# Carried-state exponents from DRAM as repeated rows, and a new order of round 2, in a fused scan and feed-forward kernel

## The chip, the cores and the metric

The kernel runs on one core of one Trainium2 chip. The metric is the device time of one execution in microseconds, as the median of several runs. TensorE does the matrix products, VectorE, ScalarE and GpSimd the element-wise work, SyncE issues DMAs. Products land in PSUM, which has eight banks of 128 x 512 floats here.

## The reference

First a gated linear recurrence in chunks over 4 batches, 8 heads, 768 steps, with head dimension 32 and state dimension 16; then a feed-forward layer with a leaky ReLU over the 3072 tokens of width 256 and inner width 2048.

```python
la = log(clip(a, 1e-6, 1));  cum = cumsum(la)            # per chunk
M = (C @ B.T) * exp(cum_i - cum_j) * causal
y = M @ x  +  (C @ state) * exp(cum_i)                   # exp(cum_i): exponents of the carried state
state = exp(sum(la)) * state + sum_j (B_j x_j) * exp(cum_last - cum_j)
h = y_as_tokens @ w_in;  out = maximum(0.01 * h, h) @ w_out
```

The kernel may choose its own chunk length; it takes 64 steps, so 12 chunks.

## The kernel before, in words

`scan_ffn` sets down every instruction in the order in which its engine runs it (`tc.manual_schedule()`): each engine goes through its own list in program order, and waits between engines follow from the tiles. Its first part is the scan, with the feed-forward work woven in; its second part is feed-forward alone.

The scan has a prologue, which makes the row sums of the decays and does chunks 0 and 1, and then rounds c = 2 to 12 (the loop `for c in range(2, NC + 1)`). Round c prepares chunk c + 1, computes the scores of chunk c and the output of chunk c - 1:

- `decays(c + 1, h)`, a product for each half h of the decay matrix, into the bank `dspace(c + 1, h)`; `decay_exp` takes its exponent on ScalarE. Up to chunk 3 the halves go to the banks `pd` and `HB[0]`, later both go to `pd`.
- `scores(c)` into the banks `pa` and `pb`; `weigh(c, half)` multiplies them on VectorE with the decays (first `pb`, then `pa`).
- `passed(c + 1)`, two products that repeat the chunk's row sums (`er`, three bf16 parts of each, through the 0/1 matrix `esel`) over the 16 state rows of each head; `passed_exp` takes their exponent on ScalarE into `es`, 128 x 256.
- `weigh_c(c + 1)` on GpSimd: `es` times C. `end_decay(c)` on GpSimd: the old state times the last exponent of the chunk. `weigh_b(c)` on GpSimd: B times its decays.
- `states(c - 1)`: the state update of a chunk; up to round 3 into `o01`, columns 128 to 191 of each of its quarters of 256, later into `pb`. `keep_state(c - 1)` copies it on VectorE in two instructions, added to `end_decay`'s product.
- `outputs(c - 1)`: y into the last 64 columns of the quarters of `pa` and `pb`. `keep_out` copies it on ScalarE (high part, two instructions), `low_out` takes the rest on VectorE (up to round 4).
- In rounds 2 and 3 there is no feed-forward product yet; `keep_warm(10, o01[:, 1, :2 * Q])` and `keep_warm(4, o01[:, 1])` put ten and four filler products without use there. From round 4 on `ffn_in(f, 0, HB[0])` and `ffn_out` stand there.
- `decode(c, part)`: the steps that turn 64-bit weights into pairs of floats: magnitude on ScalarE (L107), clamp, shift, sign and low bits on VectorE (L110, L115, L121, L127), high part on ScalarE (L133), rest on GpSimd (L136).

In round 2 VectorE moreover makes the second third of the row sums' parts (`split(1, sum1)`, four instructions), fills a slot of `dr` (`fill_slots`, L272) and copies mask rows (`mask_rows(5, NC)`, L417); ScalarE copies sign rows (`sign_rows(5, NC)`, L411). The parts are saved to DRAM (`save_sums`) and come back as rows of `dr`, `dl` and `er` (`send_rows`, `send_cols`, `send_er`).

Loads stand on SyncE's queue in program order, each as soon as its buffer is free: in every round `bs`, half of a weight (`raw`), `cs`, the other half, `ts` and `xs`.

Of the kernel before, what the change touches and what calls it, by code (L numbers as in the profile page):

```python
# [10 lines left out]
F32 = mybir.dt.float32  # L11
F32R = mybir.dt.float32r
BF16 = mybir.dt.bfloat16
U32 = mybir.dt.uint32
AF = mybir.ActivationFunctionType
# [19 lines left out]
KD = PR + 3 * GB  # L35
NE = 3 * NH
DIRECT = 2
SLOTS = 5
WARM = 6
FIRST = 4  # L40
# [9 lines left out]
def scan_ffn(ctx: ExitStack, tc: tile.TileContext, a_l, bcn_l, x_l, w_l, out_l):  # L50
# [145 lines left out]
    espace, zlate = (v[:, :, 2 * Q:2 * Q + 2 * D] for v in quarters)  # L196

    def dspace(c, h):
        return (pd, HB[0] if c < FIRST else pd)[h]

    early_q = o01.rearrange("p s (a x) -> p (s a) x", a=NH2)

    def exspace(c):
        return espace if c > 2 else early_q[:, :, (c + 1) * Q:(c + 2) * Q]
# [23 lines left out]
    dr = cst.tile([128, SLOTS, GB, Q], BF16, name="dr")  # L228
    erev = cst.tile([128, NC * GB], F32, name="erev")
    esel = cst.tile([NE, 128], BF16, name="esel")  # L230
    er = cst.tile([NE, NC * 2, CT // 2], BF16, name="er")
    parts = [cst.tile([128, 3, 2 * Q], BF16, name=f"parts{i}") for i in range(2)]
    lax = cst.tile([128, GB, N], F32, name="lax")
    reach = [p3.tile([128, GB, Q], F32, name="lt") for _ in range(DIRECT)]
# [3 lines left out]
    sel = cst.tile([128, NG, 2], F32, name="sel")  # L238
    dram = open_pool(scan, "dram", space=bass.MemoryType.DRAM)
    sums = dram.tile([NC * GB, 3, 2 * Q], BF16, name="sums")  # L240

    bs, cs, ts, xs, cms, bnd, lts, es, cds, ss, tmps = ({} for _ in range(11))

    def fetch_bc(c, which):
        if c >= NC:
            return
        for i, (d, n) in enumerate(((bs, "bs"), (cs, "cs"), (ts, "ts"))):
            if n[0] in which:
                d[c] = pin.tile([128, CT], F32, name=n)
                sp.dma_start(d[c], bcn_l[c, :, i * CT:(i + 1) * CT])  # L250

    def fetch_x(c):
        if c < NC:
            xs[c] = pin.tile([128, GB, D], F32, name="xs")
            sp.dma_start(xs[c].rearrange("p g d -> p (g d)"), x_l[c])
# [15 lines left out]
    def fill_slots(lo, hi, copy):  # L271
        copy(dr[:KD, lo:hi], dr[:KD, SLOTS - 1:].to_broadcast([KD, hi - lo, GB, Q]))  # L272

# [76 lines left out]
    def fill_reach(c, h, eng):  # L350
        lo = c * GB + h * GB // 2
        eng.tensor_tensor(
            out=reach[c][:, halves[h]],
            in0=la[:, lo:lo + GB // 2].unsqueeze(2).to_broadcast([128, GB // 2, Q]),
            in1=seen.unsqueeze(1).to_broadcast([128, GB // 2, Q]), op=ALU.mult,
        )
# [21 lines left out]
    def split(i, space):  # L378
        n = (128, 64)[i]
        p, space = parts[i][:n], space[:n]  # L380
        dve.tensor_copy(p[:, 0], space)
        dve.tensor_tensor(out=rest[:n], in0=space, in1=p[:, 0], op=ALU.subtract)
        dve.tensor_copy(p[:, 1], rest[:n])
        dve.tensor_tensor(out=p[:, 2], in0=rest[:n], in1=p[:, 1], op=ALU.subtract)
# [19 lines left out]
    def send_er(lo, hi):  # L404
# [2 lines left out]
            sums[lo * GB:hi * GB].rearrange("(c k) p i -> (k p) c i", k=NH),  # L407
        )

    def sign_rows(lo, hi):  # L410
        act.copy(  # L411
            dl[ROW:PR, lo:hi],
            sign[ROW:PR, :2].unsqueeze(1).unsqueeze(3).to_broadcast([PR - ROW, hi - lo, 2, Q]),
        )

    def mask_rows(lo, hi):
        dve.tensor_copy(  # L417
            dl[:64, lo:hi].rearrange("p c h i -> p c (h i)"),
            upto_b.rearrange("p h i -> p (h i)").unsqueeze(1).to_broadcast([64, hi - lo, 2 * Q]),
        )  # L420
# [27 lines left out]
    def weigh(c, half):  # L448
        m = lts[c].rearrange("p (a g h) i -> p a g (h i)", a=NH2, g=NG)[:, :, 2 * half:2 * half + 2]
        dve.tensor_tensor(  # L450
            out=m, in0=sspace[half].rearrange("p g a x -> p a g x"), in1=m, op=ALU.mult,
        )
# [28 lines left out]

    def end_decay(c):
        tmps[c] = pw.tile([128, NB, 2, D], F32, name="tmp")
        e = es[c].rearrange("p (q i) -> p q i", q=NB)[:, :, Q - 1:]
        pool.tensor_tensor(
            out=tmps[c].rearrange("p q h d -> p q (h d)"),
            in0=ss[c - 1].rearrange("p q h d -> p q (h d)"),
            in1=e.to_broadcast([128, NB, 2 * D]), op=ALU.mult,
        )

    def weigh_b(c):
        bnd[c] = pw.tile([128, GB, N], F32, name="bnd")
# [6 lines left out]
    def decays(c, h):  # L499
        pe.matmul(  # L500
            dspace(c, h), lhsT=dl[:KD, c].rearrange("p h i -> p (h i)"),
            rhs=dr[:KD, slot(c), halves[h]].rearrange("p g i -> p (g i)"), start=True, stop=True,
        )
# [8 lines left out]

    def passed_exp(c):
        es[c] = p3.tile([128, CT], F32, name="es")
        act.activation(es[c].rearrange("p (q i) -> p q i", q=NB), exspace(c), AF.Exp)

    def weigh_c(c):
        cds[c] = p3.tile([128, CT], F32, name="cd")
        pool.tensor_tensor(out=cds[c], in0=es[c], in1=cs[c], op=ALU.mult)

    def outputs(c):
        mt, y = lts[c], [yspace(c, m) for m in range(2)]
# [49 lines left out]
    def decode(c, part):  # L572
        for g, f in duty[c, part]:
            g(f)
# [12 lines left out]
    sign_rows(2, 5)  # L587
    spread_c(0)
    fill_slots(0, 1, act.copy)
    fill_reach(1, 0, dve)  # L590
    fill_reach(1, 1, pool)
    pool.tensor_copy(
# [44 lines left out]
    passed_exp(2)  # L637
    fetch_bc(2, "t")
    fetch_x(2)
    fetch_bc(3, "bc")  # L640
    fetch_w(0)
    fetch_bc(3, "t")
# [3 lines left out]
    for c in range(2, NC + 1):  # L646
        f = c - FIRST
        if c + 1 < NC:
            alloc_lt(c + 1)
            decays(c + 1, 0)  # L650
            decay_exp(c + 1, 0)
        if c < NC:
            scores(c)
        if c < FIRST:
            states(c - 1)
        if c + 1 < NC:
            passed(c + 1)
            passed_exp(c + 1)
            decays(c + 1, 1)
        if c < NC:  # L660
            weigh(c, 1)
            weigh(c, 0)
        if c < NC - 1:
            weigh_b(c)
        if c + 1 < NC:
            spread_c(c + 1)
            decay_exp(c + 1, 1)
            weigh_c(c + 1)
        if c == 2:
            split(1, sum1)  # L670
            fill_slots(3, 4, dve.tensor_copy)
            mask_rows(5, NC)
            decode(1, 1)
            sign_rows(5, NC)
        if f >= 0:
            low = ffn_in(f, 0, HB[0])
        else:
            keep_warm(10, o01[:, 1, :2 * Q])
        decode(c, 0)
        if c == 3:  # L680
            send_rows(5, 7)
            send_er(5, NC)
            send_cols(5, NC, sp)
        fetch_bc(c + 2, "b")
        fetch_w(c + 3 - FIRST, (0,))
        fetch_bc(c + 2, "c")
        outputs(c - 1)
        if FIRST <= c < NC:
            states(c - 1)
        keep_out(c - 1)  # L690
        if f >= 0:
            low()
        if c < NC:
            decode(c + 1, -1)
            keep_state(c - 1)
        if c < NC - 1:
            end_decay(c)
        low_out(c - 1)
        fetch_w(c + 3 - FIRST, (1,))
        if c == 2:  # L700
            save_sums(1)
        fetch_bc(c + 2, "t")
        if c in (4, 7):
            send_rows(*{4: (7, 10), 7: (10, 12)}[c])
        fetch_x(c + 1)
        if len(queue) > 1:
            ffn_out(*queue.popleft())
        elif f <= 0:
            keep_warm(4, o01[:, 1])
        decode(c, 1)  # L710
# [246 lines left out]
```

## Time and profile before

| | us |
|---|---|
| median of 3 runs | 319.48 (319.12 to 319.96) |
| the profiled execution | 318.69 |
| its span, first to last instruction | 317.0 |
| mean granted clock of TensorE | 0.994 of 2.4 GHz |

A row of the timeline gives start, duration, engine, line, operation, output and inputs, shapes and how many instructions were merged; in brackets stand the idle time of the engine just before it and what ended that. Busy shares count an engine's own instructions. The granted clock is 1.00 at 2.4 GHz and 0.50 at 1.2 GHz.

### The profile page before, as it was taken

What the parts mean: (1) busy time and instruction counts of PE and PEld (TensorE: products, weight loads), DVE (VectorE), ACT (ScalarE), POOL (GpSimd) and SP (SyncE); (2) the same over time, 40 slices, a digit from 0 to 9 for tenths busy, and PEclk for the clock granted to TensorE, in tenths of its full rate; (3) what the DMA queues carried; (4) which work ended last, traced back from release to release, by engine and by line L of the source; (5) the groups of instructions that cost most, each with busy time, mean ns of one, the idle gap of its engine ahead of it and who ended that gap; (6) DMA issues with size and microseconds to landing.
All of it is one profiled execution on the core that took longest, in us unless ns stands there. A gap on an engine that the chain in (4) does not pass through costs nothing.

```text
span 317.0 us, 7484 instructions
## 1 busy us (share of the span) xinstructions
PE 305.9 (96%) x3066; PEld 239.8 (76%) x3066; DVE 215.0 (68%) x355; ACT 190.2 (60%) x358; POOL 80.7 (25%) x110
## 2 busy tenths in 40 slices
PE   8869999999999999999999999999999999999994
PEld 3445676677888888888788888888888888888883
DVE  6575987787799997535866656766576555665541
ACT  6766887786578658544666555654375535654351
POOL 6244545653594658621000101000000000000000
PEclk9998999999999999999999999999999999999999
DMA  6758757542414000000300000000021000000003
GB/s 178 203 186 233 233 185 225 168 150 74 130 68 134 0 0 2 0 0 0 134 0 0 0 4 0 0 2 0 0 76 59 0 0 0 3 0 0 3 0 132
DMA packets 15650, 20.49 MB, mean 65 GB/s; under 512 B 3520, under 2 KB 8448, under 8 KB 15616
## 3 DMA queue, kind: packets, MB, share of 16 engines
q1 hardware_dynamic: 15456, 19.98, 20.2%
q8 instruction: 24, 0.39, 0.5%
q14 instruction: 10, 0.08, 0.1%
q10 hardware_dynamic: 160, 0.04, 0.1%
HBM read 16.72 MB, written 3.29 MB: 63 GB/s over the span
## 4 chain that ended last, share of the span: by engine, by line
PE 91%; DVE 4%; ACT 2%; issue 1%; ACTq 0%; DVEq 0%
PE o L152 40%; PE h L152 36%; PE pa L442 2%; PE pa L528 1%; PE pd L500 1%; PE pa L540 1%; PE pb L540 1%; PE pa L264 1%; PE pb L460 1%; PE o L264 1%; PE pa L507 1%; PE h L359 1%; PE pd L359 1%; ACT gh L865 1%; PE pb L442 1%
## 5 line engine op out<-in xcount | busy, mean ns | idle before, releaser
L865 ACT ACTIVATE gh<-tmp 128x512 fp32r<-128x512 f32 x48 | 30.2, 629 | 49.6 <-DVE tmp L889 46.3
L867 DVE TENSOR_TENSOR gl<-tmp,gh 128x512 fp32r<-128x512 f32 x48 | 33.2, 692 | 21.8 <-ACT tmp L866 21.8
L152 PE MATMUL o<-gh,wha 128*128 128x512 f32 x120 | 47.6, 397 | 0.0
L152 PE MATMUL o<-gh,wla 128*128 128x512 f32 x120 | 46.8, 390 | 0.0
L152 PE MATMUL o<-gl,wha 128*128 128x512 f32 x120 | 46.7, 389 | 0.0
L186 DVE TENSOR_TENSOR gl<-h,gh 128x512 fp32r<-128x512 f32 x32 | 22.0, 688 | 15.1 <-ACT h L184 14.6
L866 ACT ACTIVATE tmp<-tmp 128x512 f32<-128x512 f32 x48 | 30.4, 633 | 1.5
L183 ACT ACTIVATE gh<-h 128x512 fp32r<-128x512 f32 x32 | 19.1, 595 | 16.9 <-PE h L152 16.9
L152 PE MATMUL o<-gh,whb 128*128 128x512 f32 x72 | 28.0, 389 | 0.0
L152 PE MATMUL o<-gh,wlb 128*128 128x512 f32 x72 | 28.0, 389 | 0.0
L152 PE MATMUL o<-gl,whb 128*128 128x512 f32 x72 | 28.0, 389 | 0.0
L152 PEld LDWEIGHTS o<-gh,wha 128*128 128x128 f32 x120 | 22.5, 188 | 5.1
L152 PEld LDWEIGHTS o<-gl,wha 128*128 128x128 f32 x120 | 22.5, 188 | 4.8
L152 PEld LDWEIGHTS o<-gh,wla 128*128 128x128 f32 x120 | 22.5, 188 | 4.4
L152 PE MATMUL h<-oph,wsh 128*128 128x512 f32 x64 | 24.9, 389 | 0.0
L152 PE MATMUL h<-oph,wsl 128*128 128x512 f32 x64 | 24.9, 389 | 0.0
L152 PE MATMUL h<-opl,wsh 128*128 128x512 f32 x64 | 24.9, 389 | 0.0
L884 DVE TENSOR_TENSOR tmp<-h,tmp 128x512 f32<-128x512 f32 x16 | 11.1, 691 | 20.4 <-PE h L152 20.4
L882 ACT COPY tmp<-h 128x512 f32<-128x512 f32 x16 | 9.4, 588 | 20.8 <-PE h L152 20.8
L184 ACT ACTIVATE h<-h 128x512 f32<-128x512 f32 x32 | 19.0, 593 | 0.0
L136 POOL TENSOR_TENSOR wla<-w,wha 128x512 fp32r<-128x512 f32 x10 | 12.9, 1287 | 23.5 <-ACT wha L133 23.5
L426 ACT ACTIVATE lt<-pd 128x512 f32<-128x512 f32 x20 | 11.9, 593 | 10.1 <-PE pd L500 7.9
(174 smaller groups left out, 716.6 us busy)
## 6 DMA issues: line engine op xcount, KB each, us to landing
raw<-w_l SPq DMA_DIRECT2D x32, 256.0 KB, 3.5
xs<-x_l SPq DMA_DIRECT2D x12, 256.0 KB, 3.8
out_l<-ob SPq DMA_DIRECT2D x9, 256.0 KB, 2.0
bs<-bcn_l SPq DMA_DIRECT2D x12, 128.0 KB
cs<-bcn_l SPq DMA_DIRECT2D x12, 128.0 KB, 3.3
ts<-bcn_l SPq DMA_DIRECT2D x12, 128.0 KB, 3.0
out_l<-wtmp SPq DMA_DIRECT2D x3, 256.0 KB
la<-a_l SPq DMA_DIRECT2D x1, 96.0 KB
```

The source lines that it names most:

```text
L136: (eng or dve).tensor_tensor(out=weight(1, f), in0=w32(f), in1=weight(0, f), op=ALU.subtract)
L152: pe.matmul(space, lhsT=w, rhs=x, start=start and i == 0, stop=stop and i == 2, skip_group_check=again,)
L183: act.activation(gh, hp, AF.Prelu, alpha=0.01)
L184: act.activation(hp, hp, AF.Prelu, alpha=0.01)
L186: return lambda: dve.tensor_tensor(out=gl, in0=hp, in1=gh, op=ALU.subtract)
L426: act.activation(lts[c][:, halves[h]], dspace(c, h).rearrange("p (g i) -> p g i", i=Q), AF.Exp)
L442: pe.matmul(sspace[g // 2][64 * st:64 * st + 64, g % 2, bp].rearrange("p (h i) -> p h i", h=2), lhsT=bs[c][r, cols], rhs=cms[c][r, :, cols ...
L865: act.activation(gh, v, AF.Prelu, alpha=0.01)
L866: act.activation(v, v, AF.Prelu, alpha=0.01)
L867: return g, lambda: dve.tensor_tensor(out=gl, in0=v, in1=gh, op=ALU.subtract)
L882: act.copy(a, A)
L884: dve.tensor_tensor(out=u2, in0=B, in1=a, op=ALU.add)
```

## The change

Exponents from chunk 5 on (`STACKED = 5`) are taken before they are repeated: `exp_rows(0)` in the prologue and `exp_rows(1)` in round 2 exponentiate all row sums on ScalarE, 128 x 128 and 64 x 128; `save_exp` writes them to a DRAM tensor `esums`, and `fetch_exp(c + 2)` loads them from round 3 on, with two transfers for each chunk, whose source repeats the row of a head over its 16 state rows. `passed` and `passed_exp` run for chunks up to 4 alone. The columns of `es` stand in another order (batch pair outside), so `passed_exp`, `weigh_c` and `end_decay` view them with other strides. The second half of chunk 4's decays goes to `HB[0]`.

In rounds 2 and 3 `keep_state(c - 1)` follows `weigh` directly, on VectorE's list ahead of `split` and in program order ahead of the ten fillers. In round 2 `sign_rows`, the magnitude, clamp, shift and sign passes of weight 0 and `mask_rows` go behind `low_out(1)`, in this order.

```diff
+STACKED = 5
     def dspace(c, h):
-        return (pd, HB[0] if c < FIRST else pd)[h]
+        return (pd, HB[0] if c <= FIRST else pd)[h]
-    er = cst.tile([NE, NC * 2, CT // 2], BF16, name="er")
+    er = cst.tile([NE, STACKED * 2, CT // 2], BF16, name="er")
+    erow = [cst.tile([128, 2 * Q], F32, name=f"erow{i}") for i in range(2)]
+    esums = dram.tile([NC * GB, 2 * Q], F32, name="esums")
+    def exp_rows(i, space):
+        n = (128, 64)[i]
+        act.activation(erow[i][:n], space[:n], AF.Exp)
+
+    def save_exp(i):
+        n = (128, 64)[i]
+        sp.dma_start(esums[i * 128:i * 128 + n], erow[i][:n])
+
+    def fetch_exp(c):
+
+        if STACKED <= c < NC:
+            es[c] = p3.tile([128, CT], F32, name="es")
+            for b in range(NH2):
+                rows = esums[c * GB + b * NH:c * GB + (b + 1) * NH].unsqueeze(1)
+                sp.dma_start(
+                    es[c][:, b * 2 * Q:(b + 1) * 2 * Q], rows.to_broadcast([NH, N, 2 * Q])
+                )
+    def by_part(v):
+        return v.rearrange("p (b s i) -> p s b i", b=NH2, s=2)
     def end_decay(c):
-        e = es[c].rearrange("p (q i) -> p q i", q=NB)[:, :, Q - 1:]
+        e = by_part(es[c])[:, :, :, Q - 1:].to_broadcast([128, 2, NH2, 2 * D])
     def weigh_c(c):
-        pool.tensor_tensor(out=cds[c], in0=es[c], in1=cs[c], op=ALU.mult)
+        pool.tensor_tensor(out=out, in0=by_part(es[c]), in1=c_in, op=ALU.mult)
     fill_slots(0, 1, act.copy)
+    exp_rows(0, o01[:, 0, :2 * Q])
     fetch_x(2)
+    save_exp(0)
     for c in range(2, NC + 1):
-        if c + 1 < NC:
+        if c + 1 < STACKED:
             passed(c + 1)
             passed_exp(c + 1)
+        if c + 1 < NC:
             decays(c + 1, 1)
         if c < NC:
             weigh(c, 1)
             weigh(c, 0)
+        if 1 < c < FIRST:
+            keep_state(c - 1)
         if c == 2:
             split(1, sum1)
+            exp_rows(1, sum1)
             fill_slots(3, 4, dve.tensor_copy)
-            mask_rows(5, NC)
-            decode(1, 1)
-            sign_rows(5, NC)
         if f >= 0:
             low = ffn_in(f, 0, HB[0])
         else:
             keep_warm(10, o01[:, 1, :2 * Q])
-        decode(c, 0)
+        if c > 2:
+            decode(c, 0)
         if c == 3:
             send_rows(5, 7)
-            send_er(5, NC)
         if c < NC:
             decode(c + 1, -1)
+        if FIRST <= c < NC:
             keep_state(c - 1)
         low_out(c - 1)
+        if c == 2:
+            sign_rows(5, NC)
+            decode(1, 1)
+            decode(2, 0)
+            mask_rows(5, NC)
         if c == 2:
             save_sums(1)
+            save_exp(1)
+        if c >= 3:
+            fetch_exp(c + 2)
```

## Rows read from the trace of the kernel before

**Rows 1.** The page: busy time of each engine, and the last chain by engine.

```profile
PE 305.9 (96%) x3066; PEld 239.8 (76%) x3066; DVE 215.0 (68%) x355; ACT 190.2 (60%) x358; POOL 80.7 (25%) x110
...
PE 91%; DVE 4%; ACT 2%; issue 1%; ACTq 0%; DVEq 0%
```

**Rows 2.** TensorE's timeline, rounds 2 to 4: start, duration, line, output, inputs, count, idle.

```profile
16.04 0.39 PE L500 MATMUL pd<-dr,dl 118*128 118x512 bf16 x1
...
17.59 0.39 PE L500 MATMUL h<-dr,dl 118*128 118x512 bf16 x1
17.81 0.72 PE L264 MATMUL o<-idle 128*128 128x128 bf16 x10
18.95 0.27 PE L528 MATMUL pa<-cd,ss 32*64 32x64 f32 x2 [0.41 <-POOL cd L519]
...
22.81 1.56 PE L264 MATMUL o<-idle 128*128 128x512 bf16 x4 [1.92 <-DVE ss L472]
...
28.00 0.27 PE L528 MATMUL pa<-cd,ss 32*64 32x64 f32 x2 [0.36 <-DVE lt L450]
...
29.42 1.04 PE L264 MATMUL o<-idle 128*128 128x512 bf16 x4
30.29 0.38 PE L500 MATMUL pd<-dr,dl 118*128 118x512 bf16 x1
```

**Rows 3.** VectorE's timeline, rounds 2 and 3.

```profile
18.71 0.25 DVE L381 CAST parts<-sum 64x128 bf16<-64x128 f32 x1
...
19.78 0.41 DVE L272 COPY dr<-dr 118x1024 bf16<-118x1024 bf16 x1
20.11 0.60 DVE L417 COPY dl<-upto_b 64x896 bf16<-64x896 bf16 x1
...
21.55 0.69 DVE L121 SCALAR_TENSOR_TENSOR w<-raw,w 128x512 uint32<-128x512 uint32 x1
22.16 0.60 DVE L472 SCALAR_TENSOR_TENSOR ss<-o,odd,tmp 128x128 f32<-128x128 f32 x2
...
27.26 0.69 DVE L450 TENSOR_TENSOR lt<-pa,lt 128x512 f32<-128x512 f32 x1 [0.58 <-ACT es L515]
```

**Rows 4.** Windows of 0.25 us: stretch, length, busy time by engine, clock, DMA.

```profile
core 0: us, PE busy (x) PEld busy (x) DVE busy (x) ACT busy (x) POOL busy (x), PEclk, DMA share, GB/s
23.00:23.25 0.25, 0.25 (x2) 0.10 (x1) 0.25 (x2) 0.00 (x0) 0.25 (x1) 0.81 0.80 295
26.50:26.75 0.25, 0.25 (x3) 0.11 (x4) 0.18 (x1) 0.00 (x0) 0.00 (x0) 0.87 0.80 148
```

**Rows 5.** TensorE's timeline, end of the prologue: `passed(2)`.

```profile
15.83 0.28 PE L507 MATMUL o<-er,esel 24*128 24x128 bf16 x2 [0.95 <-DVE xl L560]
```

**Rows 6.** ScalarE's timeline, round 2.

```profile
19.25 0.68 ACT L107 ACTIVATE w<-raw 128x512 f32<-128x512 f32 x1
19.95 0.93 ACT L411 COPY dl<-sign 6x896 bf16<-6x896 bf16 x1
20.90 0.37 ACT L550 CAST xh<-pa 128x256 fp32r<-128x256 f32 x1
```

**Rows 7.** Timelines of ScalarE and TensorE, rounds 5 and 6.

```profile
36.16 0.60 ACT L426 ACTIVATE lt<-pd 128x512 f32<-128x512 f32 x1 [0.17 <-PE pd L500]
37.46 0.28 PE L507 MATMUL pa<-er,esel 24*128 24x128 bf16 x2
43.03 0.60 ACT L426 ACTIVATE lt<-pd 128x512 f32<-128x512 f32 x1 [0.79 <-PE pd L500]
43.54 0.28 PE L507 MATMUL pa<-er,esel 24*128 24x128 bf16 x2
43.76 0.39 PE L500 MATMUL pd<-dr,dl 118*128 118x512 bf16 x1
```

**Rows 8.** DMA issues and their landing (page), and timelines of SyncE and GpSimd.

```profile
raw<-w_l SPq DMA_DIRECT2D x32, 256.0 KB, 3.5
43.00 0.38 SPq L250 DMA_DIRECT2D ts<-bcn_l  x1
50.46 0.75 POOL L519 TENSOR_TENSOR cd<-es,cs 128x256 f32<-128x256 f32 x1 [0.39 <-ACT es L515]
```

More of the change, by code (lines that the diff above doesn't have):

```diff
@@ L483, in end_decay @@
         tmps[c] = pw.tile([128, NB, 2, D], F32, name="tmp")
-        e = es[c].rearrange("p (q i) -> p q i", q=NB)[:, :, Q - 1:]
[L485 to L488, printed above, removed]
-        )
+        out, old = (
+            v.rearrange("p (s b) h d -> p s b (h d)", s=2) for v in (tmps[c], ss[c - 1])
+        )
+        e = by_part(es[c])[:, :, :, Q - 1:].to_broadcast([128, 2, NH2, 2 * D])
+        pool.tensor_tensor(out=out, in0=old, in1=e, op=ALU.mult)
     def weigh_b(c):
@@ L514, in passed_exp @@
         es[c] = p3.tile([128, CT], F32, name="es")
-        act.activation(es[c].rearrange("p (q i) -> p q i", q=NB), exspace(c), AF.Exp)
+        act.activation(
+            by_part(es[c]), exspace(c).rearrange("p (s b) i -> p s b i", s=2), AF.Exp
+        )
     def weigh_c(c):
         cds[c] = p3.tile([128, CT], F32, name="cd")
-        pool.tensor_tensor(out=cds[c], in0=es[c], in1=cs[c], op=ALU.mult)
+        out, c_in = (v.rearrange("p (s b i) -> p s b i", s=2, b=NH2) for v in (cds[c], cs[c]))
+        pool.tensor_tensor(out=out, in0=by_part(es[c]), in1=c_in, op=ALU.mult)
     def outputs(c):
```

## Prediction

> **What bounds the kernel now.** I read the page first: TensorE is busy for 96% of the span, and 91% of the chain that ended last is TensorE [rows 1]. So a microsecond is worth something only where the chain leaves TensorE or where TensorE's own queue gets shorter. Behind the scan (rounds 2 to 12) the change touches nothing; I take that stretch as shifted, not altered. The second view is TensorE's timeline of rounds 2 and 3. The reader is to see one hole: the ten filler products of round 2 end at 18.53, `outputs(1)` starts at 18.95, and the four fillers behind it start only at 22.81, after 1.92 us of nothing, released by the state copy on VectorE (L472) [rows 2]. The third view, VectorE's timeline, says why: that copy stands behind the four passes of `split`, the slot copy, the mask copy and three weight passes, from 18.71 to 22.16 [rows 3]. The fourth is the granted clock in quarter microseconds: it falls to half inside the slice 23.00 to 23.25 (mean 0.81) and is back inside 26.50 to 26.75 (0.87), which places the fall at 23.15 and the return at 26.57: 3.4 us at 1.2 GHz, begun 0.3 us after TensorE had resumed [rows 4].
>
> **The change part by part.**
>
> Round 2's state copy goes to 18.71, where `split` starts now, and ends 0.60 later, at 19.31 [rows 3]. But in the new order it also stands ahead of the ten fillers, which write the bank `o01[:, 1]` that the copy reads. Their columns differ (0 to 127 against 128 to 191). A case of just this is in the trace: at 15.83 the products of `passed(2)`, which write columns 192 to 255 of `o01`'s quarters, waited 0.95 us for the VectorE pass that reads columns 0 to 127 [rows 5]. So I let the fillers wait. The Trainium skill (PSUM — Partial Sum Buffer, PSUM bank collisions raise a hardware error) asks for PSUM to be guarded by bank and quadrant and not by address; by that rule the fillers wait, the trace agrees, and reading by columns alone they would not, which is a rival below. The copy to the fillers takes 0.05 us (22.76 to 22.81) [rows 2, 3], so they start at 19.36 instead of 17.81, take 0.72, and `outputs(1)` starts at 20.1 instead of 18.95 [rows 2].
>
> From there TensorE is quick: `outputs` to the four fillers 1.42 and these to the next `decays` 0.87 (28.00, 29.42, 30.29), so `decays(4, 0)` at 22.4; from the first `decays` of a round to the second 1.55 (16.04 to 17.59); the second now has the bank `HB[0]` and waits for no exponent: 23.9, ended 24.3 [rows 2]. Then come ten fillers again, and they are now behind round 3's state copy. So VectorE decides. Y's second half is copied by ScalarE from 21.55 to 21.9 (0.37); `sign_rows` follows with 0.95 (19.95 to 20.90) and only then the magnitude pass L107 with 0.68: 23.5 [rows 6]. VectorE's clamp waits for that; clamp, shift, sign and mask copy are the four passes that now run from 20.11 to 22.16, 2.05: 25.6. Two `weigh` passes of 0.69 follow, then the copy of 0.60: 27.5 [rows 3]. The 0.58 us that `weigh` waited for the carried exponents at 27.26 is gone, as these now come early; what is late instead is the weight work in front of it [rows 3]. Fillers at 27.5, `outputs(2)` at 28.2. Now it starts at 28.00 [rows 2]. The reorder thus buys nothing at this point; I count +0.2. Bounds: 0.5 less if VectorE's passes overlap at their ends as they do in the rows and ScalarE takes Y a little sooner, 0.3 more if GpSimd's product of chunk 4 slows the copies beside it.
>
> What does change is where TensorE stands idle: 24.3 to 27.5, 3.2 us, where it was 1.92. The shorter hole was followed by a fall to half clock [rows 2, 4], so I expect one here. In the kernel before, its price is already inside the 28.00. Now it falls on the fillers, `outputs(2)` and the four fillers behind, 0.72 + 1.42 + 0.87 = 3.0 us of work back to back which opens round 4. Slowed as the four fillers were (1.56 against 1.04, a factor of 1.5 [rows 2]), 3.4 us at half clock lose 1.1. Bounds: 0 if the stretch lies in the hole, 1.7 if every cycle in it counts. I take +1.1.
>
> Rounds 4 to 10 lose `passed` and `passed_exp` (seven pairs of products, seven exponents). On TensorE a pair takes 0.22 (43.54 to 43.76) [rows 7]. But the `decays` product behind it writes the single bank `pd`, which ScalarE is still reading: L426 runs from 43.03 to 43.63 [rows 7]. With 0.05 to wake, `decays` can start at 43.68 instead of 43.76: 0.08 of the 0.22, and the exponent of the first half is next to be late. In round 5 L426 is done at 36.76 and the pair would start at 37.46, so there all 0.22 come out [rows 7]. Sum: 6 x 0.08 + 0.22 = 0.7. Bounds: 0.2 (only round 5) and 1.5 (all seven whole). ScalarE's exponent in each round lies off the path.
>
> Costed at nothing: the two `exp_rows` (the first has ScalarE idle behind it, the second stands in front of Y's copy, which waits for TensorE); the two `save_exp`; `weigh_c` and `end_decay` with another stride, on GpSimd, which is busy for 25% of the span [rows 1]. The fourteen `fetch_exp` transfers stand on SyncE's queue ahead of `ts` and `xs`. That queue works a round ahead: the load of chunk 8's `ts` goes out at 43.00, chunk 8's product on GpSimd runs at 50.46, and a weight load of 256 KB lands 3.5 us after its issue [rows 8]. Some 4 us of cover; if it went, GpSimd's product would be late first, not TensorE.
>
> Sum: +0.2 + 1.1 - 0.7 = +0.6 on the profiled execution's 318.69 us (span 317.0 and 1.69 around it), 319.3. That execution lies 0.79 below the median of the runs, so I forecast 319.48 + 0.6 = 320.1.
>
> **The rivals.**
>
> A. The fillers don't wait for the copy. Then `outputs(1)` stays at 18.95 and ends at 20.89, 0.6 before my 21.5; VectorE's chain moves up by that, and `outputs(2)` waits for `weigh` alone, without copy and fillers (1.3): 26.3, 1.9 below mine: 318.2. For it: the columns are disjoint. Against it: [rows 5]. Chance 0.12.
>
> B. The fall to half clock doesn't come, or lies in the hole: 1.1 less, 319.0. For it: in this kernel a fall lagged the hole by 0.3 us after the work resumed, so its place isn't fixed by the order. Against it: the hole is 1.3 us longer than the one that was followed by a fall. Chance 0.17.
>
> C, the slower side: the new hole in round 2, 17.98 (end of the `decays` at 17.59) to 19.36, 1.4 us, is followed by half clock too. A hole of 0.95 before 15.83 was not, one of 1.92 was [rows 2, 5]; this lies between. `outputs(1)` would then take half as long again, +0.7, and the chain over Y's copy, `sign_rows`, L107 and the four passes hands all of it on, with the fillers' 0.4: 321.2. It decides from where `outputs(1)` ends after 21.5, since ScalarE has no slack between Y and L107. Chance 0.18.
>
> D. The loads of repeated rows come late. The row says 3.5 us to landing for 256 KB [rows 8]. The Trainium skill (DMA: Bandwidth & Descriptors, Rules for kernel authors) says that a pattern whose outermost dimension is below 16 confines a transfer to that many engines; these sources start with 8 heads. No run here shows it yet. If the time to landing doubles to 7, chunk 8's exponents land about when GpSimd wants them; only beyond 9 to 10 us would its later product of weights, and with it TensorE, be late. Six rounds by up to 0.4: 322.5. Chance 0.04.
>
> **How the numbers follow.** My case has 0.45, A 0.12, B 0.17, C 0.18, D 0.04; 0.04 I leave for instruction-fetch pauses on TensorE that move. My case alone gives 319.2 to 321.2: the bounds of the reorder, the half clock and the rounds partly cancel. The range goes from A's 318.1 to C with its bound, 322.0, and leaves D and the outer ends of A out. 0.3% is 0.96 us, about what a measurement of this kernel can tell from no change: faster means below 318.52, slower above 320.44. Faster: most of A, a little of B and of my case, 0.19. Slower: most of C and D and a third of my case, 0.35. The rest, 0.46, is no difference.
>
> **What would show it.** In the profile after: the ten fillers of round 2 released by L472 at about 19.4 (if they run at 17.8, A holds); `outputs(1)` at 20.1; L107 on ScalarE behind `sign_rows`, ending near 23.5; TensorE idle from 24.3 to 27.5 with the state copy as releaser; half clock for about 3.4 us from somewhere between 26 and 29; `decays(5, 0)` between 31 and 32 instead of 30.29; in the rounds from 6 on, TensorE released by L426 ahead of the second `decays`, and rounds shorter by under 0.1 us. I'm wrong if `outputs(2)` starts well before 28, or if the rounds shorten by 0.2 each.

## The result and the profile after

| | before | changed |
|---|---|---|
| median | 319.30 (317.51 to 319.96, 4 runs) | 322.16 (321.57 to 322.92, 4 runs) |
| profiled execution | 318.69 | 321.96 |
| its span | 317.0 | 320.2 |
| mean granted clock | 0.994 | 0.989 |

The changed kernel takes 1.0100 times as long (95%: 1.0053 to 1.0147). That is 2.9 us slower, where 0.6 was forecast; the median lies 2.1 above the forecast 320.1 and just above the range. The kernel before has one run more than the three of the forecast's base. Ratios, here and below, leave out single executions that took over 1.5% longer than the fastest of their kernel, and they are not the quotient of the two medians beside them (e7: 319.65 against 319.54, ratio 0.9981).

In the listing of the changed kernel the lines stand lower: `decays` L500 is L523, `outputs` L528 and L540 are L554 and L566, the fillers L264 are L267, `weigh` L450 is L474, `keep_state` L472 is L496, `decay_exp` L426 is L450, `sign_rows` L411 is L435, the magnitude L107 is L108, the sign pass L121 is L122, the FFN products L152 are L153.

The page, busy time and last chain, beside [rows 1]: TensorE has no more work than before, the span has 3.2 us more.

```profile
PE 306.0 (96%) x3052; PEld 240.6 (75%) x3052; DVE 216.0 (67%) x355; ACT 188.2 (59%) x353; POOL 80.3 (25%) x110
...
PE 90%; DVE 4%; ACT 3%; issue 1%; ACTq 0%; DVEq 0%
```

TensorE's timeline of rounds 2 to 4, beside [rows 2]. The landmarks I use from here on are the first `decays` product of a round: 15.88 (chunk 3), 23.55 (chunk 4) and 33.52 (chunk 5).

```profile
15.88 0.39 PE L523 MATMUL pd<-dr,dl 118*128 118x512 bf16 x1
...
17.54 0.39 PE L523 MATMUL h<-dr,dl 118*128 118x512 bf16 x1
19.32 1.22 PE L267 MATMUL o<-idle 128*128 128x128 bf16 x10 [1.39 <-DVE ss L496]
...
22.65 1.07 PE L267 MATMUL o<-idle 128*128 128x512 bf16 x4
23.55 0.38 PE L523 MATMUL pd<-dr,dl 118*128 118x512 bf16 x1
...
25.08 0.39 PE L523 MATMUL h<-dr,dl 118*128 118x512 bf16 x1
29.26 0.97 PE L267 MATMUL o<-idle 128*128 128x128 bf16 x10 [3.79 <-DVE ss L496]
...
32.35 1.33 PE L267 MATMUL o<-idle 128*128 128x512 bf16 x4
33.52 0.38 PE L523 MATMUL pd<-dr,dl 118*128 118x512 bf16 x1
```

Two holes, both ended by the state copy, where [rows 2] had one; and ten fillers that took 0.72 there take 1.22 and 0.97. The windows of the granted clock (columns as in [rows 4]) say why:

```profile
19.25:19.50 0.25, 0.18 (x3) 0.18 (x3) 0.21 (x3) 0.24 (x2) 0.16 (x1) 0.67 0.71 270
19.50:22.50 3.00, 3.00 (x106) 2.66 (x104) 1.75 (x4) 0.18 (x1) 1.09 (x2) 0.50 0.13 34
22.50:22.75 0.25, 0.25 (x16) 0.11 (x2) 0.03 (x1) 0.19 (x1) 0.00 (x0) 0.51 0.27 69
...
29.50:29.75 0.25, 0.25 (x7) 0.25 (x5) 0.25 (x1) 0.00 (x0) 0.00 (x0) 0.65 0.57 174
29.75:32.75 3.00, 3.00 (x103) 2.24 (x102) 0.39 (x2) 1.29 (x4) 2.21 (x3) 0.50 0.84 233
32.75:33.00 0.25, 0.25 (x2) 0.15 (x1) 0.24 (x2) 0.25 (x2) 0.25 (x2) 0.53 0.70 229
```

TensorE runs at 1.2 GHz twice for 3.4 us, behind each of the two holes, and both times it is busy throughout (3.00 of 3.00). Before there was one such stretch [rows 4].

ScalarE, GpSimd and VectorE in round 3, beside [rows 3, 6]:

```profile
23.15 0.93 ACT L435 COPY dl<-sign 6x896 bf16<-6x896 bf16 x1
24.11 0.67 ACT L108 ACTIVATE w<-raw 128x512 f32<-128x512 f32 x1
24.81 0.43 DVE L111 TENSOR_SCALAR w<-w 128x512 f32<-128x512 f32 x1 [1.23 <-ACT w L108]
...
25.70 0.73 POOL L545 TENSOR_TENSOR cd<-es,cs 128x256 f32<-128x256 f32 x1 [5.11 <-ACT es L538]
25.73 1.24 DVE L122 SCALAR_TENSOR_TENSOR w<-raw,w 128x512 uint32<-128x512 uint32 x1
26.90 0.60 DVE L441 COPY dl<-upto_b 64x896 bf16<-64x896 bf16 x1
...
28.62 0.59 DVE L496 SCALAR_TENSOR_TENSOR ss<-o,odd,tmp 128x128 f32<-128x128 f32 x2
```

The magnitude waits for the sign rows, as forecast. The sign pass takes 1.24 instead of 0.69 [rows 3]: GpSimd's product for chunk 4 (L545) runs beside its first half.

A steady round, from the chain of the stretch 30 to 60 (start, duration, what), beside [rows 7]: the second `decays` product is released by ScalarE's exponent, and the round lasts 5.98 (45.91 to 51.89), 0.10 less than before (42.60 to 48.68).

```profile
46.34 0.61 ACT lt L450
46.95 0.04 issue
...
52.32 0.61 ACT lt L450
```

Behind round 3 the two profiles agree: from the first `decays` of chunk 5 to the end 286.7 us in both. The whole loss lies between the landmarks of chunk 3 and chunk 5: 17.64 us, before 14.25.

### The profile page after: what moved, and what is told of

The parts are those of the page before. It is cut to its first block, busy times and chain, and to the rows that moved or that the text cites. A ratio compares the mean times of both kernels' runs of the same rounds, so it can differ in the third digit from the quotient of the medians.

```text
span 320.2 us, 7450 instructions
## 1 busy us (share of the span) xinstructions
PE 306.0 (96%) x3052; PEld 240.6 (75%) x3052; DVE 216.0 (67%) x355; ACT 188.2 (59%) x353; POOL 80.3 (25%) x110
## 4 chain that ended last, share of the span: by engine, by line
PE 90%; DVE 4%; ACT 3%; issue 1%; ACTq 0%; DVEq 0%
PE o L153 40%; PE h L153 36%; PE pa L554 2%; PE pd L523 1%; PE o L267 1%; PE pa L566 1%; PE pb L566 1%; PE pa L466 1%; PE pa L267 1%; PE pb L484 1%; ACT lt L450 1%; PE h L362 1%; PE pd L362 1%; DVE lt L474 1%; ACT gh L903 1%
## 5 line engine op out<-in xcount | busy, mean ns | idle before, releaser
L153 PE MATMUL o<-gh,wha 128*128 128x512 f32 x120 | 47.6, 397 | 0.0
L153 PE MATMUL o<-gl,wha 128*128 128x512 f32 x120 | 46.7, 389 | 0.0
L153 PE MATMUL o<-gh,wla 128*128 128x512 f32 x120 | 46.7, 389 | 0.0
L153 PE MATMUL o<-gh,whb 128*128 128x512 f32 x72 | 28.0, 389 | 0.0
L153 PE MATMUL o<-gh,wlb 128*128 128x512 f32 x72 | 28.0, 389 | 0.0
L153 PE MATMUL o<-gl,whb 128*128 128x512 f32 x72 | 28.0, 389 | 0.0
L153 PEld LDWEIGHTS o<-gh,wha 128*128 128x128 f32 x120 | 22.5, 188 | 5.2
L153 PEld LDWEIGHTS o<-gl,wha 128*128 128x128 f32 x120 | 22.5, 188 | 4.7
L153 PEld LDWEIGHTS o<-gh,wla 128*128 128x128 f32 x120 | 22.5, 188 | 4.4
L153 PE MATMUL h<-oph,wsh 128*128 128x512 f32 x64 | 24.9, 389 | 0.0
L153 PE MATMUL h<-oph,wsl 128*128 128x512 f32 x64 | 24.9, 389 | 0.0
L153 PE MATMUL h<-opl,wsh 128*128 128x512 f32 x64 | 24.9, 389 | 0.0
L153 PE MATMUL h<-xh,wha 128*128 128x512 f32 x40 | 17.1, 427 | 0.0
```

The source lines that it names most:

```text
L153: pe.matmul(space, lhsT=w, rhs=x, start=start and i == 0, stop=stop and i == 2, skip_group_check=again,)
```

## The experiments

Two theories stood at the start. Order (O in the expectations): the new order of rounds 2 and 3 costs the time, through two idle stretches with the half clock behind each (theory C later on) and through the weight passes. Loads (L): the loads, or the missing products, cost it. Each run is read by its median against the kernel before on the same chip, and by the landmarks of its profile ("the stretch" is that from chunk 3's landmark to chunk 5's). Pauses are pieces of 0.1 us and more that the chain calls issue, between 30 and 95: an engine, mostly TensorE, waits for nothing that the profile shows. I take them for instructions that come late; no run shows that.

**e1, loads alone.** The order of the kernel before.

```diff
-        if 1 < c < FIRST:
-            keep_state(c - 1)
...
             fill_slots(3, 4, dve.tensor_copy)
+            mask_rows(5, NC)
+            decode(1, 1)
+            sign_rows(5, NC)
...
-        if FIRST <= c < NC:
+        if c < NC:
             keep_state(c - 1)
```

> The exponents loaded as repeated rows, but rounds 2 and 3 in the order of the kernel before and chunk 4's second half in pd as before. Theory O (order): the whole loss sits in rounds 2 and 3, so this kernel is between 0 and 0.7 us faster than before, 318.6 to 319.3; decays(5, 0) at about 30.3 as before. Theory L (loads): the transfers cost more than the removed products give, through pauses in TensorE's instruction fetch or late data, so this kernel is slower than before by 0.5 us or more, 319.8 or above.

Median 320.60 against 318.87, ratio 1.0033 (0.9995 to 1.0071). From chunk 3 to chunk 5 12.76 us, with the clock at 1.00 from 18 to 40, although TensorE stood idle for 2.03 us before the four fillers: such a hole was followed by half clock in the kernel before and not here. It came later: from 40.33 on, again for 3.4 us, behind a wait of 0.51 and a pause of 1.26. No gain from the loads, and by the interval no certain loss.

**e2, order alone.** The products of the kernel before for all chunks; the edit is against the kernel before.

```diff
+        if 1 < c < FIRST:
+            keep_state(c - 1)
...
-            mask_rows(5, NC)
-            decode(1, 1)
-            sign_rows(5, NC)
...
+        if c == 2:
+            sign_rows(5, NC)
+            decode(1, 1)
+            decode(2, 0)
+            mask_rows(5, NC)
```

> The new order of rounds 2 and 3 with chunk 4's second half in HB[0], but every chunk's exponents by products as before. Theory O: decays(5, 0) at 33 to 33.6 as in the changed kernel, two stretches at half clock, and the whole time 2.9 to 3.9 us above before, 322.2 to 323.2. Theory L: less than half of the loss, 319.8 to 320.8.

321.30 against 318.87, ratio 1.0063 (1.0027 to 1.0099): the order alone makes the kernel slower. The median lies between what the two theories expected, with some two thirds of the changed kernel's loss (0.63 of 1.00%); whether the rest is more than chance the intervals don't tell. From chunk 3 to chunk 5 it is 17.18 us, nearly as in the changed kernel (17.64), but of other parts: the half clock of round 2 lasts 6.8 us, the hole of round 3 is 2.21, and the sign pass takes 0.69.

**e3, fillers ahead of the state copy** in program order, so that they have nothing to wait for.

```diff
+        if f < 0:
+            keep_warm(10, o01[:, 1, :2 * Q])
         if c < NC:
             weigh(c, 1)
```

> The changed kernel with the ten fillers of rounds 2 and 3 in program order directly behind the second decays, so ahead of the state copy. Theory O: fillers at 17.8 instead of 19.32, outputs(1) at about 19 instead of 20.47, no half clock in round 2, outputs(2) at about 26.4 instead of 30.17, then one stretch at half clock that costs about 1; decays(5, 0) at 29.3 to 30.3 and the whole time 3 to 4 us below the changed kernel, 318.0 to 319.2. If the fillers' place is not what costs (ScalarE's and VectorE's order alone does), it gains under 1.5: 320.7 or above.

320.26, ratio 1.0019 (0.9982 to 1.0056). The fillers run without a wait, round 2 shows no half clock, and the stretch is 15.24 us, in spite of a pause of 1.32 on TensorE. Round 3 keeps a hole, 2.72 ended by `weigh`, with half clock behind it. Most of the loss is gone; the median is 1 us worse than expected.

**e4, magnitude ahead of the sign rows** on ScalarE.

```diff
         if c == 2:
+            decode(1, 1)
             sign_rows(5, NC)
-            decode(1, 1)
```

> The changed kernel with weight 0's magnitude pass ahead of the sign rows on ScalarE (0.95 us earlier). Theory O: the fillers of round 3 and all behind them come 0.95 earlier (fillers at 28.3 instead of 29.26), whole time 321.2 against 322.2. If VectorE is held by something else in that stretch, under 0.3 us of gain.

321.39, ratio 1.0069 (1.0037 to 1.0102); the stretch is 16.51, 1.1 shorter. Half clock in both rounds, as in the changed kernel, but in round 2 for 6.8 us.

**e5, holes filled.** The order stays; TensorE gets something to do.

```diff
         else:
+            keep_warm({2: 19, 3: 50}[c], pd[:, :2 * Q])
             keep_warm(10, o01[:, 1, :2 * Q])
```

> The changed kernel with more fillers (the same 128x128 products, 0.072 us each at the full clock), 19 in round 2 and 50 in round 3, written to the bank pd, which nothing else needs just then, ahead of the ten that wait for the state copy. They lie in the two idle stretches of TensorE that the changed kernel shows (1.39 us at 17.93, 3.79 us at 25.47) and wait for nothing themselves. Theory C (the two stretches at the half clock, 19.33 to 22.74 and 29.58 to 33.0, follow from these two idle stretches, and cost 0.50 on the fillers, 0.76 on outputs(1) and 1.06 on outputs(2) and the four fillers): the granted clock stays at 1.00 from 18 to 33, the ten fillers last 0.72, and decays(5,0) starts 15.2 to 15.8 us after decays(3,0), not 17.64; median 319.5 to 320.3. Theory W (the lateness is that of the state copies and the weight passes, and the clock only fills what is a wait anyway): decays(5,0) starts 17 us or more after decays(3,0) although the clock is full, and the median is 321.5 or more.

320.95, ratio 1.0065 (1.0027 to 1.0103). TensorE's timeline:

```profile
18.62 0.72 PE L267 MATMUL o<-idle 128*128 128x128 bf16 x10 [0.33 <-DVE ss L496]
...
21.22 1.04 PE L267 MATMUL o<-idle 128*128 128x512 bf16 x4
22.10 0.38 PE L523 MATMUL pd<-dr,dl 118*128 118x512 bf16 x1
...
27.81 0.72 PE L267 MATMUL o<-idle 128*128 128x128 bf16 x10 [0.96 <-DVE ss L496]
...
29.88 1.04 PE L267 MATMUL o<-idle 128*128 128x512 bf16 x4
30.75 0.38 PE L523 MATMUL pd<-dr,dl 118*128 118x512 bf16 x1
```

The ten fillers take 0.72 again in both rounds, all ten executions show a mean clock of 0.997 to 1.000, and the stretch is 15.46 us instead of 17.64, as theory C expected. So products that nobody reads took 2.2 us off it. The median gave only about half of that, and missed the expected 319.5 to 320.3: the profiled execution has 2.62 us of pauses behind round 3, the changed kernel's had 1.36, which may be the reason.

**e6, both single steps and fillers:** e3 and e4 together, with 6 and 22 more fillers into `pd`.

```diff
+            keep_warm({2: 6, 3: 22}[c], pd[:, :2 * Q])
```

> The changed kernel with both single steps together: the ten fillers of a round ahead of the state copy, as in e3, and the magnitude pass ahead of the sign rows on ScalarE, as in e4; and behind the ten fillers 6 more in round 2 and 22 more in round 3, into the bank pd, so that TensorE is not idle for the rest of the hole. If the losses of rounds 2 and 3 are separate terms (the idle stretches with the half clock behind them, and the magnitude pass behind the sign rows, 1.1): decays(5,0) starts 13.1 to 14.0 us after decays(3,0) (15.24 in e3, 16.51 in e4, 17.64 in the changed kernel, 14.25 before), and the median is 318.0 to 319.2. If the weight passes hold keep_state(2) and outputs(2) whatever the order (the rival), decays(5,0) stays 15 us or more behind and the median is that of e3, 320.3.

319.17 against 319.54, ratio 0.9997 (0.9960 to 1.0035). The stretch is 13.99, of which 1.25 are a wait for a load of `dl`. The loss of the new order is gone, as was expected if its terms are separate ones.

**e7, transfers alone:** the products stay, the loads go to a tile that nothing reads.

```diff
+            spare = cst_es
+            for b in range(NH2):
...
+                sp.dma_start(
+                    spare[:, b * 2 * Q:(b + 1) * 2 * Q], rows.to_broadcast([NH, N, 2 * Q])
+                )
```

> The kernel before, with its products and its order, and the transfers of the change added: the exponents' rows to DRAM and two loads of 64 KB per chunk from chunk 5 on, into a tile that nothing reads; and the two small exponents on ScalarE (0.3 each). What is measured is the price of the transfers and their issue alone. Theory F (the loads cost TensorE time through pauses in which it waits for its own instructions: 0.65 and 0.11 us in the kernel before and 0.45 in the one without loads, 0.98 to 2.5 in the four with loads): such pauses add up to 1.0 us or more between 30 and 92, and the median is 319.4 to 320.4 against 318.9 before. Theory N (the transfers are free, and what the pauses show is chance): the median is within 0.3 of that of the kernel before, with pauses of 0.8 or less.

319.65 against 319.54, ratio 0.9981 (0.9944 to 1.0017), pauses 0.76: the transfers cost nothing that can be measured.

**e8, the kernel before with its hole filled.**

```diff
         outputs(c - 1)
+        if c == 2:
+            keep_warm(26, pd[:, :2 * Q])
```

> The kernel before with 26 more fillers in round 2 between outputs(1) and the four fillers that wait 1.92 us for the state copy, into the bank pd. Theory C: the stretch at the half clock behind that wait (mean granted clock 0.86 between 18 and 30) goes; decays(5,0) starts 13.0 to 13.6 us after decays(3,0), not 14.25; median 317.7 to 318.3 against 318.9. Theory W: the wait for the exponents (lt, 0.36 ahead of outputs(2)) and the weight passes take the place of what the clock gives: the median moves by less than 0.3.

319.12 against 319.54, ratio 0.9983 (0.9949 to 1.0018). The clock is 1.00 from 18 to 30, the stretch 12.77 instead of 14.25: the half clock was there to be had. The median moved by 0.4, too little to tell, and short of the 0.6 to 1.2 that theory C expected. The landmarks of chunks 3 and 5:

```profile
17.80 0.39 PE L500 MATMUL pd<-dr,dl 118*128 118x512 bf16 x1
...
30.57 0.38 PE L500 MATMUL pd<-dr,dl 118*128 118x512 bf16 x1
```

Beside e5 this prices the order by itself. With the clock at 1.00 throughout, the stretch is 15.46 in the new order and 12.77 in the old one: 2.7 of the 3.4 us by which it grew are the new order itself, its waits and VectorE's slower passes, and 0.7 is the half clock (2.2 in the changed kernel, 1.5 before). These are single profiles, but the loads make no difference in them: e9, below, takes 12.87.

**e9, e8 with the loads in place of the products, and e10, e6 with the products in place of the loads.** Each is the other half of a pair.

> The loads of the change with the order of the kernel before, and with the 26 fillers of e8 in round 2, so that TensorE's clock does not fall there; to be read against e8, the same fillers with the products. If the step on the loads holds (a steady round 0.08 to 0.10 shorter, seven rounds, nothing given back): decays(5,0) 12.8 us after decays(3,0) as in e8, rounds of 5.98 instead of 6.08, and a median 0.5 to 0.8 below that of e8 (which stood 0.4 below the kernel before), so 0.9 to 1.2 below the kernel before. Rival (the pauses in which TensorE waits for its instructions are longer where the products are gone: 0.98 to 2.62 on the chain from 30 to 95 in six kernels with loads and no products, 0.45 to 1.86 in four with products): the rounds are shorter all the same, pauses of 1.4 or more, and a median level with e8 or above.

> The kernel e6 (new order, ten fillers ahead of the state copy, more fillers into pd, magnitude ahead of the sign rows) with the products of the kernel before for the exponents of chunks 5 on. Step on the loads: rounds of 6.08, median 0.5 to 0.8 above e6, so level with the kernel before or up to 0.5 over it. Rival as in e9: pauses below 1.0 and a median level with e6 or below.

e9: 318.99 against 319.19, ratio 0.9986 (0.9955 to 1.0016), pauses 2.11. e10: 318.38, ratio 0.9972 (0.9936 to 1.0008), pauses 0.30, the lowest median of all, though not told apart from the kernel before. Its stretch lasts 12.85.

In both pairs, and in e1 against before, the kernel with loads has the higher ratio: by 0.33, 0.03 and 0.25%, in the mean by 0.20% (-0.06 to 0.46, the intervals taken together). The forecast was -0.2%. Neither median of e9 and e10 came as the step on the loads had it. This spoke for the rival, longer pauses; e13 to e16 test it.

**e11, weight passes back ahead of outputs(1),** with the early state copy and the loads.

```diff
         if c == 2:
             split(1, sum1)
+            mask_rows(5, NC)
+            decode(1, 1)
+            sign_rows(5, NC)
```

> The changed kernel with the weight passes and sign rows of round 2 back ahead of outputs(1), where the kernel before has them; the early state copy and the loads stay. It tells apart the two halves of the new order. If the early state copy alone costs the time (fillers wait for it, the idle stretch and the half clock behind): the first idle stretch stays near 1.4 us and decays(4,0) is late as in the changed kernel, but from decays(4,0) to decays(5,0) it is 6.1 to 6.6 us (6.12 before, 9.97 in the changed kernel, 8.17 with the magnitude pass first); decays(5,0) 13.8 to 15.2 us after decays(3,0); median 319.3 to 320.5. If the moved weight passes are innocent: decays(5,0) 16.5 us or more after decays(3,0), median 321.5 or more.

319.88 against 319.19, ratio 1.0023 (0.9994 to 1.0052), inside the expectation. The stretch is 14.42, of which 6.55 from chunk 4 to chunk 5:

```profile
19.79 1.06 PE L267 MATMUL o<-idle 128*128 128x128 bf16 x10 [1.39 <-DVE ss L496]
...
22.96 1.24 PE L267 MATMUL o<-idle 128*128 128x512 bf16 x4
24.04 0.38 PE L523 MATMUL pd<-dr,dl 118*128 118x512 bf16 x1
...
27.61 0.72 PE L267 MATMUL o<-idle 128*128 128x128 bf16 x10 [1.44 <-DVE ss L496]
...
29.71 1.04 PE L267 MATMUL o<-idle 128*128 128x512 bf16 x4
30.59 0.38 PE L523 MATMUL pd<-dr,dl 118*128 118x512 bf16 x1
```

The first hole is still followed by half clock (fillers 1.06), the second, now 1.44, is not. So the early state copy only exchanges one hole with half clock behind it for another. The 2.1 us between e11 and the changed kernel belong to the moved weight passes: they make the second hole 3.79 and bring the second stretch.

**e12, the changed kernel once more.**

> The changed kernel itself once more, beside the others on this chip, for a second profile of it: whether both idle stretches are followed by the half clock again. If the two stretches belong to the kernel: decays(5,0) 17.2 to 18.0 us after decays(3,0), mean clock 0.98 to 0.99, median 321.2 to 322.4. If one of them is a matter of the single execution: decays(5,0) 16.0 to 16.9 us after decays(3,0) in this profile, and a median of 320.2 to 321.2.

Ratio 1.0091 (1.0058 to 1.0124). Two of its ten executions, the profiled one among them, took more than twice as long and are left out of the comparison; so it gave no second profile. The other eight have a mean clock of 0.979 to 0.995; the one at 0.995 took 321.76, hardly less than the rest (320.87 to 324.96). That fits e5 and e8: the half clock is not the larger part of the loss.

**e13 to e16.** e13 is e9 without the loads as well; from chunk 5 on it reads ones. e14 is e9 with two idle products of the pair's size in the pair's place.

```diff
-            es[c] = p3.tile([128, CT], F32, name="es")
-            for b in range(NH2):
...
+            es[c] = fixed
```

```diff
+            for st in range(2):
+                pe.matmul(
+                    espace[:, st * NH2:(st + 1) * NH2], lhsT=idle[:24, :128],
...
         if c + 1 < NC:
             decays(c + 1, 1)
```

> The kernel e9 without the fourteen loads: chunks from 5 on read a tile of ones instead of their exponents, so the kernel has neither the products nor the loads (what it leaves out is the decay of the carried state from chunk 5 on). It tells what the longer instruction pauses of TensorE hang on. Theory T (they hang on the 64 KB loads): pauses on the chain from 30 to 95 add up to 1.0 us or less, as in the kernels with products (0.30 to 1.86, mean 0.87 of five), and the median is 0.7 to 1.2 below that of the kernel before. Theory P (they hang on TensorE's queue being shorter without the products): pauses of 1.4 to 2.6 (0.98 to 2.62, mean 1.95, in the eight kernels with loads and without products) and a median within 0.5 of the kernel before.

> The kernel e9 with loads, and with two products of the removed pair's size (24x128 by 128 columns, of zeros, read by nobody) put back where the pair stood, so that TensorE's queue is as long as before while ScalarE's exponents stay away. Rounds of 6.08 again if the pair costs its place, 5.98 if it runs in the wait for ScalarE. Theory P: pauses below 1.0 and a median at or below that of e9. Theory T: pauses of 1.4 or more, as in e9 (2.11), and a median at e9's or above.

> The kernel before, for a second profile of it beside these two. If pauses belong to a kernel: 0.8 to 1.2 on the chain from 30 to 95 (1.00 in its first profile), decays(5,0) 14.0 to 14.4 us after decays(3,0). If they are a matter of the single execution, they are elsewhere and may well be twice as long or nearly none.

> The changed kernel, for the second profile of it that e12 didn't give. If both idle stretches are followed by the half clock as a property of the kernel: decays(5,0) 17.2 to 18.0 us after decays(3,0). If it is a matter of the single execution: 16.0 to 16.9. Pauses on the chain from 30 to 95: 1.0 to 2.6 if they belong to kernels without the products (1.36 in its first profile), below 0.9 if they are chance.

e13: 318.75 against 319.43, ratio 0.9983 (0.9947 to 1.0020), pauses 1.90 where theory T wanted 1.0 or less; its median, 0.7 below, is close to what T had (0.7 to 1.2). e14: 318.90, ratio 0.9993 (0.9958 to 1.0028), a round of 6.07, so the pair costs its place; pauses 2.46 where theory P wanted less than 1.0. So neither the loads nor the shorter queue alone lengthens the pauses, as far as one profile each can tell. e15, the kernel before: pauses of 2.43 where its first profile had 1.00, and a stretch of 13.23, less than the 14.0 expected, as the clock stays at 1.00 in it. Its chain's larger pieces from 30 to 60, and the one behind:

```profile
33.13 0.54 issue
...
42.34 0.34 issue
...
55.41 0.38 issue
...
61.59 0.54 issue
```

The first lies between two passes of VectorE; with three shorter pieces, 1.17 of the 2.43 are not TensorE's own. TensorE's part is 1.26, and 0.76 in the first profile. So the pauses differ between executions of one kernel, and a single profile settles nothing about them. And e15 set against the other executions of the very same kernel came out at 0.9967 (0.9938 to 0.9996): two sets of one kernel differ by 0.33%. Differences of this size, those of the pairs above among them, say nothing.

e16, the changed kernel: 322.82, ratio 1.0123 (1.0084 to 1.0162), and a second profile:

```profile
18.79 1.23 PE L267 MATMUL o<-idle 128*128 128x128 bf16 x10 [1.39 <-DVE ss L496]
...
28.58 1.23 PE L267 MATMUL o<-idle 128*128 128x128 bf16 x10 [3.79 <-DVE ss L496]
```

17.36 us from chunk 3 to chunk 5, both holes of the same length and followed by half clock again. They belong to the kernel.

## Why the prediction was wrong

Between the profiled executions, the forecast was 318.69 + 0.6 = 319.3; it was 321.96, 2.66 more. By the landmarks, forecast and measured:

| stretch | forecast | measured | difference |
|---|---|---|---|
| first `decays` of chunk 3 to the fillers of round 2 | 3.32 | 3.44 | +0.12 |
| these to the first `decays` of chunk 4 | 3.04 | 4.23 | +1.19 |
| this to the fillers of round 3 | 5.10 | 5.71 | +0.61 |
| these to the first `decays` of chunk 5 | 4.10 | 4.26 | +0.16 |
| change of the rest, to the end | -0.70 | -0.03 | +0.67 |
| change of what lies ahead and around | 0 | -0.09 | -0.09 |

**Right:** the fillers wait for the state copy (forecast 19.36, in the trace 19.32, and 1.39 for the 1.4 us hole), so rival A is out. The magnitude behind the sign rows, VectorE as the one that releases `outputs(2)`, a hole longer than 3 us in round 3 and half clock behind it that falls on work: all there, the last at 4.26 instead of 4.10. Rival B is out. The steady round is 0.10 shorter, 0.08 was forecast, with ScalarE's exponent as the new releaser. Rival D is out too. The pair of loads takes SyncE 1.22 us to issue, but GpSimd never waits for it:

```profile
46.47 1.22 SPq L427 DMA_DIRECT2D es<-esums  x2
...
52.49 0.80 POOL L516 TENSOR_TENSOR bnd<-ts,erev 128x256 f32<-128x256 f32 x1
53.26 0.74 POOL L545 TENSOR_TENSOR cd<-es,cs 128x256 f32<-128x256 f32 x1
```

L545 follows L516 without a gap.

**The step that failed** is the one that held the hole of round 2 to be too short for the half clock. The text had the question as rival C, between a hole of 0.95 that was not followed by it and one of 1.92 that was [rows 2, 5], and gave it 0.18. The hole of 1.39 was followed by half clock in each of the five profiles that show it (the changed kernel twice, e2, e4, e11): 1.19 us in the table, forecast as 1.1 by C. With the hole filled, in e5, the clock stays at 1.00 and the same piece takes 3.48, of which 0.30 are a pause. Two rows, one on either side of 1.4, gave no reason for a chance far from one half; I had let the main case take no fall as if the rows had said so. With C in the sum, and the 0.7 of the rounds left out, the same working gives 321.9 against the 322.16 measured. That is luck in part: from the profiled execution's 318.69 it gives 321.1, and 321.96 was measured, mostly since VectorE's passes are missing in it.

**A term that was mis-sized:** VectorE's passes in round 3, +0.61. I took 2.05 for the four from [rows 3] and 0.3 as the bound for GpSimd beside them. They took 2.69, and 0.55 of the 0.64 is the sign pass, the one that reads two SBUF tiles. GpSimd's product is the cause: where it runs beside that pass, it takes 1.16 to 1.24 (the changed kernel twice, e3, e5), and 0.69 in the four of the new order where it doesn't (e2, e4, e6, e10). The same is to be seen in round 2, where the two passes of `split` that took 0.28 and 0.22 before run beside GpSimd now:

```profile
19.34 0.62 POOL L512 TENSOR_TENSOR tmp<-ss,es 128x256 f32<-128x256 f32 x1 [0.51 <-DVE ss L496]
19.42 0.68 DVE L385 TENSOR_TENSOR rest<-sum,parts 64x128 f32<-64x128 f32 x1
19.92 0.67 POOL L516 TENSOR_TENSOR bnd<-ts,erev 128x256 f32<-128x256 f32 x1
20.14 0.53 DVE L386 CAST parts<-rest 64x128 bf16<-64x128 f32 x1
```

**A gain that didn't reach the end:** the 0.7 of rounds 4 to 10. In an undisturbed round it is there (5.98 against 6.08). Round 5, from which 0.22 were forecast, gave none (6.98 from landmark to landmark, before 6.86). From chunk 5's landmark to chunk 11's it is 37.37 us, before 37.71; behind it 0.31 of these 0.34 are lost again, where a pause of 0.55 stands (0.11 before). I had put the loss to the missing products first, then to the loads; e13 and e14 speak against either alone. What is left is this: counted on TensorE alone, the pauses add up to 0.3 to 1.9 us (mean 0.9) in the six profiles with the exponents' products throughout, and to 1.0 to 2.5 (mean 1.9) in the eleven without. Pauses longer by 1.0 would more than take back the 0.7. That is argued from groups of kernels that differ in other things too, and no run shows what makes a pause. Whether a tenth per round reaches the end stays open: it is 0.2%, and two sets of one kernel differed by 0.33%.

So the change is slower by its order, and by that of the weight passes above all (e11: 2.1 of the 2.9 us). Filling the holes takes part of that back (e5), and all of it together with moving two steps (e6). The loads in place of the products bring neither a sure gain nor a sure loss (0.20%, -0.06 to 0.46).

## What to carry to other kernels

Price a new idle stretch of TensorE with what stands behind it: here a hole of 1.4 us mostly put the next 3.4 us or more at 1.2 GHz, which cost about 1.2 us in the changed kernel, nearly as much as the hole itself; idle products into a bank that nobody needs took that back without moving anything else. But price the new order's own waits and passes first: here they were 2.7 us, and the additional half clock 0.7. When passes are moved, ask what runs beside them at the new place, GpSimd above all. And a gain of 0.1 us per round is not to be forecast as time if executions of one kernel differ by more than its sum.

## What the runs showed of the hardware

- The half clock is no fixed answer to a hole's length. The hole of 1.39 was followed by it five times out of five, one of 1.44 in round 3 once (e4) and once not (e11), and the holes in round 2 of the order before not always: 1.92 yes (before), 0.86 behind a pause of 1.31 yes (e7), 2.03 no (e1), 1.48 behind a pause of 0.69 no (e15). In these rounds it lasted 3.4 us each time, but 6.8 in round 2 of e2 and e4. Where the clock falls isn't fixed either: for the hole of 1.39 it fell 1.3 us before the fillers in e2, 0.7 before them in e4, and at 19.33 in the first profile of the changed kernel, as they start. In the second it fell about 0.4 us before they do:

```profile
18.00:18.25 0.25, 0.00 (x0) 0.00 (x0) 0.25 (x2) 0.25 (x2) 0.25 (x1) 1.00 0.57 205
18.25:18.50 0.25, 0.00 (x0) 0.00 (x0) 0.25 (x2) 0.25 (x2) 0.04 (x1) 0.72 0.57 176
```

- TensorE pauses, without a wait that the profile shows, for 0.3 to 2.5 us in sum between 30 and 95, in pieces of up to 1.4 (1.36 in e11). The sum changes from execution to execution of one kernel: 0.76 and 1.26 before, 1.36 and 2.01 in the changed one.
- The scan's start differs by 2 us, in one and the same kernel: the first `decays` of chunk 3 stood between 15.3 and 16.5 or between 17.7 and 18.1 in all profiles, in the kernel before at 16.04 and at 18.11 (e15). TensorE's first fillers run at half their later pace (two take 1.03 in e15's prologue, four take 1.04 in its round 3), and that lasts longer in some executions; the granted clock reads 1.00 over all of it. TensorE's timeline of the prologue, first of the kernel before, then of e15:

```profile
5.96 0.65 PE L264 MATMUL pa<-idle 128*128 128x512 bf16 x2
6.45 1.02 PE L359 MATMUL pd<-lt,after 128*128 128x512 f32 x2
```

```profile
5.96 1.03 PE L264 MATMUL pa<-idle 128*128 128x512 bf16 x2
6.79 1.91 PE L359 MATMUL pd<-lt,after 128*128 128x512 f32 x2
```

- VectorE's sign pass (128 x 512, two SBUF inputs) took 0.69 alone and 1.16 to 1.24 with GpSimd at work beside it. The Trainium skill (SBUF — State Buffer, Who interferes with whom) says that a VectorE instruction with two inputs in SBUF contends with a GpSimd instruction that reads SBUF; the trace agrees.
